# RWKV-7 state scan and hash-routed experts on one core: identity taken out of u, own and ends moved to GpSimd, routing moved to the last ticks

## The chip, the core and the metric

The kernel runs on one NeuronCore of a Trainium2 chip. A core has five engines with queues of their own: TensorE (PE in the profile, with its weight loads as PEld), VectorE (DVE), ScalarE (ACT), GpSimd (POOL) and SyncE (SP, which here only issues DMA transfers). Each works through its instructions in order; an instruction that waits holds everything behind it on the same engine. The metric is device time in microseconds; smaller is better.

## What is computed

An RWKV-7 recurrence over 768 steps for 4 x 8 heads of size 40, then an expert layer in which each token goes to one of eight experts by a hash of its id.

```python
for t in range(S):
    y[:, :, t] = np.einsum('bhd,bhde->bhe', rt, state)
    Sa = np.einsum('bhde,bhe->bhd', state, at)
    state = state * wt[:, :, None, :] - np.einsum('bhd,bhe->bhde', Sa, bt)
    state = state + np.einsum('bhd,bhe->bhde', vt, kt)
...
expert_idx = token_ids * 2654435761 % E
for e in range(E):
    mask = expert_idx == e
    out[mask] = np.maximum(x[mask] @ w1[e], 0.0) @ w2[e]
```

The state starts at zero. x is y with the heads of a token side by side: 3072 tokens of 320 values. Everything is float32.

## The kernel before

**Tiles.** The sequence is cut into 12 chunks of 64 steps. A tile is one chunk of two of the four batches: 24 tiles, numbered u, alternating between two states (g = u mod 2). Partitions 0-63 hold one batch's 64 steps, 64-127 the other's. Inside a chunk the recurrence is solved by matrix products. Products of w (the decays) scale a, b, k and r; a_ps holds the products of a with b and k; a unit triangular 64 x 64 system per head is inverted. It is split in two blocks of 32 (BLK): the diagonal blocks of four tiles (a group) are inverted together on DVE, column by column (31 steps of two instructions, outer and ub), and the off-diagonal block comes from two small matmuls, x (from ut, a transposed copy of the inverse) and u (from ug, another one).

**The order.** Each piece of work is a function with a tick, a number. The plan is sorted by tick and emitted in that order; an order written by hand decides each engine's queue. Tile u is prepared at ticks up to u+1 (tile_a: loads, multiplication by decays, transposes z_ps and t_ps, a_ps) and finished at tick u + LAG, LAG being 8 (tile_m, tile_s, tile_b). Within a tick the steps are c, u, rcc, nc, rcv, z, s, a, sd, x, r0, at_t, r1, y, rv. So one tick finishes tile k and prepares tile k+8; from tile 16 on only finishing is left.

**The steps that matter here.**
- x_ps (tile_m) goes to xi by ACT. xi also holds a 32 x 32 identity, written once at the start (L212), so that the u matmul, with 64 stationary columns, gives both the off-diagonal block and a copy of ug. ACT copies u_ps to um (L647) and writes the first half of um as ug times the mask first (L651).
- c_ps = r1 times um; cv is its copy (ACT, L721); rc needs cv; ACT's copy rv (L687) stands ahead of cv. nc transposes cv and gives x_all (L749).
- r0 (tile_b) adds the old state sc to r1; s adds it to the new state through an identity matmul, y adds it through sd. DVE makes sc from s_ps (L765), mr from rc_ps (L738), xs from y_ps (L782). For the first tile of each state sc and sd are zero, set on POOL (L166).
- Matmul results lie in PSUM: two buffers in turn (psa) for c, rc, z, a, sd and the transposes, two others (psb) for u, nc, s, x, r1, y, ex, en. A step waits until the reader of the step two before it in its pair is done.
- The decays are made in rounds (ri) of two chunks by decays(): clamp (L302, DVE), prefix and suffix products (on POOL from round 1), own (L312, L314: the product of a half chunk, DVE), ex_ps (PE: exchange of halves), ends (L334, DVE), recip (L341), spread (L345, POOL), and the transposes qt and pt (L349, DVE).
- routing() is a generator called in steps from tick 11.5 on, 0.42 apart: load of the token ids (tok, L828), counts by two matmuls (sums_ps), ranks and slots on DVE, 24 indirect scatters into slot_dram (POOL, L910), the read back to idx_all, and src_all on DVE. The first gather of the expert stage needs src_all and all x_rows.
- py (the decay product per row) is loaded and x_rows stored on POOL's queue, except the stores of the last two tiles, which are on SP.

Of the kernel before, what the change touches and what calls it, by code (L numbers as in the profile page):

```python
# [18 lines left out]
def kernel(  # L19
# [13 lines left out]
    nc = tc.nc  # L33
# [141 lines left out]
    for lo, hi, when in ((0, 4, -9.0), (4, NZ, -3.0)):  # L175
        @at_tick(when)
        def _(lo=lo, hi=hi):
            nc.gpsimd.memset(z_all[:, lo:hi].rearrange("p i b hp (two x) -> p (i b hp two) x", two=2)[:, :, D:C], 0.0)
# [8 lines left out]
    r_r = ring("r", 2, [P, HP, P], gaps)  # L187
    x_all = hold.tile([P, 3, 2, HP, P], F32, name="x_all")
    @at_tick(-3.0)
    def _():  # L190
        nc.gpsimd.memset(x_all[:].rearrange("p i b hp (two x) -> p (i b hp two) x", two=2)[:, :, D:C], 0.0)
    e2_r = ring("e2", 2, [P, R], lambda t: t.rearrange("p (two x) -> p two x", two=2)[:, :, D:C], 1)
    sd_r = ring("sd", NG, [R, 2, HP, 2, D], all_of)
    sc_r = ring("sc", NG, [R, 2, HP, 2, C], all_of)
    pend_r = ring("pend", NR, [P, RN, NG, 2, HP, 2], all_of, NR)
    nk = hold.tile([P, LAG, 2, 2, HP, C], F32, name="nk")
    xi_r = ring("xi", 1, [P, H, C])
# [9 lines left out]

    @at_tick(-8.95)
    def _():
        for be in range(2):  # L210
            rows = slice(be * C + BLK, (be + 1) * C)
            nc.scalar.copy(xi_r(0)[rows, :, BLK:C], ident[rows, rows].unsqueeze(1).to_broadcast([BLK, H, BLK]))  # L212
# [67 lines left out]
    def decays(ri, t_load, t_clamp, t_chain, t_own, t_ex, t_ends, t_pair, t_recip, t_en, t_spread, t_turn):  # L280
# [3 lines left out]
        chain = nc.vector if fast else nc.gpsimd  # L284

        for i in range(4 * RN):
            @at_tick(t_load + (0.06 * i if ri > 2 else 0))
            def _(i=i):
# [6 lines left out]
                eng = nc.scalar if fast and n % 2 else nc.sync  # L295
                r0 = (y * RN + n) * NG * H
                dma = eng.dma_start(x["pb"][r0:r0 + NG * H], src)
# [11 lines left out]
        def own():  # L309
            p, q = segs(x["pb"]), segs(x["qb"])  # L310
            x["own"] = own = work.tile([P, SEG, D], F32, tag="own", name="own", bufs=2)
            nc.vector.tensor_tensor(own[:], p[:, :, SL - 1], q[:, :, SL - 1], op=OP.mult)  # L312
            for s in range(SEG - 2, -1, -1):
                nc.vector.tensor_tensor(own[:, s], own[:, s], own[:, s + 1], op=OP.mult)  # L314
# [17 lines left out]
        def ends():  # L332
            ends = x["ends"]
            nc.vector.tensor_tensor(ends[:, 0:SEG], x["own"][:], ends[:, SEG].unsqueeze(1).to_broadcast([P, SEG, D]), op=OP.mult)  # L334
# [113 lines left out]
    def tile_a(u):  # L448
# [8 lines left out]
        if early:  # L457
            t_in, t_inz = -8.9 + 0.01 * u, -8.9 + 0.01 * u if u < 3 else -8.45
            t_mul = -6.0 + 0.01 * u
            t_mulz = -6.1 + 0.01 * u if u < 2 else t_mul - 0.005  # L460
            t_z, t_at, t_a = u - 0.3, (-0.15, 0.5, 0.95, 1.0)[u], u + 0.9 if u < 3 else u + 0.4
# [70 lines left out]
        def _():  # L532
# [9 lines left out]
            if u > GRP - 2:  # L542
                nc.scalar.copy(both, p[:])  # L543
                for be in range(2):
                    low = slice(be * C + BLK, (be + 1) * C)
                    nc.scalar.copy(nk[low, u % LAG, :, 0, :, 0:BLK], p[low, :, 0:HP * C].rearrange("p two (hp t) -> p two hp t", hp=HP)[..., BLK:])
# [24 lines left out]
    def group_i(gi, t0, t1, t2, t3):  # L571
# [38 lines left out]
        @at_tick(t3, order=9)  # L610
        def _():
            ub = x["u"]
            x["ug"] = ug = work.tile([P, BLK, BLK], F32, tag="ug", name="ug", bufs=1)
            nc.vector.transpose(ug[:].rearrange("p g t -> p t g"), ub[:].rearrange("p s t -> p t s"))
# [5 lines left out]
    def tile_m(u, t0):  # L620
# [5 lines left out]
        def _():  # L626
# [7 lines left out]
            for be in range(2):  # L634
                low = slice(be * C + BLK, (be + 1) * C)
                nc.scalar.copy(xi[low, :, 0:BLK], p[low])

        @at_tick(t0 - 1, "u")
        def _():
            ug, xi = groups[gi]["ug"], x["xi"]  # L640
            p = bank([P, H, BLK], "u_ps")
            for hp, par, be in quarters():
                h = hx(par, hp)
                low = slice(be * C + BLK, (be + 1) * C)
                mm(p[half(be), h, :], xi[low, h, :], ug[low, ti * H + h, :])
            x["um"] = um = work.tile([P, H, C], F32, tag="um", name="um", bufs=1)
            nc.scalar.copy(um[:, :, BLK:C], p[:])  # L647

        @at_tick(t0 - 0.7 if u else t0 - 0.93)
        def _():  # L650
            nc.scalar.mul(x["um"][:, :, 0:BLK], groups[gi]["ug"][:, ti * H:(ti + 1) * H, :], first[:, 0:1])  # L651

    def tile_s(u, t0):
# [20 lines left out]
        def _():  # L674
            x["py"] = py = work.tile([P, DM], F32, tag="py", name="py", bufs=1)
            cols = slice((rn * NG + g) * H, (rn * NG + g + 1) * H)
            nc.gpsimd.dma_start(py[:], p_dram[ri][:, cols].rearrange("t c e -> t (c e)"))
# [11 lines left out]
    def tile_b(u, t0):  # L689
# [5 lines left out]
        @at_tick(*((t0 - 1, "r0") if u else (6.56,)))  # L695
        def _():
            x["r1_ps"] = p = bank([P, DM], "r1_ps")
            for hp in range(HP):
                for be in range(2):
                    c0 = hp * 2 * D  # L700
                    mm(p[half(be), c0:c0 + 2 * D], x["at_t"][0:R, be, hp, :], st[:, be, hp, :, 0:D],
                       start=hp == 0, stop=False)

        @at_tick(*((t0 - 1, "r1") if u else (6.57,)))
        def _():
            p = x.pop("r1_ps")
            for hp, par, be in quarters():
# [3 lines left out]
                   start=False)  # L711
# [39 lines left out]
        if not last:  # L751
            @at_tick(t0, "s")
            def _():
# [3 lines left out]
                for par in range(2):  # L757
                    mm(p[half(par)], ident[half(par), half(par)], sc[half(par), :, :, par, 0:D], stop=False)
                for hp, par, be in quarters():
                    mm(p[half(par), be, hp * D:(hp + 1) * D], x["z"][:, be, hp, half(par)], x["x"][:, be, hp, half40(par)],  # L760
                       start=False)
# [8 lines left out]
        def _():  # L770
            p = bank([P, DM], "y_ps")
            for hp in range(HP):
# [4 lines left out]
            for hp, par, be in quarters():  # L777
                c0 = (2 * hp + par) * D
                mm(p[half(be), c0:c0 + D], x["mr"][:, par, hp * 2 + be, :],
                   x["z"][:, be, hp, par * C:par * C + D], start=False)  # L780
            xs = work.tile([P, DM], F32, tag="xs", name="xs", bufs=1)
            nc.vector.tensor_tensor(xs[:], p[:, 0:DM], x["py"][:], op=OP.mult)  # L782
            for be in range(2):
                r0 = batch(g, be) * S + n * C
                (nc.sync if last else nc.gpsimd).dma_start(x_rows[r0:r0 + C, :], xs[half(be)])  # L785
# [14 lines left out]
    decays(1, -8.5, -7.09, (-7.08, -7.0), 0.85, 0.91, 0.92, 1.2, 0.93, 3.6, 0.95, (3.445, 2.0))  # L800
    decays(2, -5.5, 3.45, (5.61, 5.9), 6.2, 6.555, 6.56, 6.57, 6.561, 8.2, 6.58, (7.62, 7.55))
    for ri in range(3, NR):
        t = ri * RN * NG
        decays(ri, t - 5.8, *((7.75, (8.3, 8.9), 8.95) if ri == 3 else (t - 5.2, (t - 5.1, t - 3.9), t - 3.55)), t - 2.9, t - 2.89, t - 2.6, t - 2.45, t - 1.88, t - 2.4, (t - 0.9, t - 1.48))
# [5 lines left out]
    for gi in range(NU // GRP):  # L810
# [3 lines left out]
        else:  # L814
            group_i(gi, t0 + 0.03, t0 + 0.06, t0 + 2.68, t0 + 2.97)
# [126 lines left out]
    for i in range(14 + TPP):  # L942
        at_tick(11.5 + 0.42 * i, order=7)(lambda: next(steps, None))
# [287 lines left out]
```

## Time and profile before

| | us |
|---|---|
| runs | 716.06, 719.69, 712.3 (median 716.06) |
| the profiled execution | 702.85 |
| its span, first to last instruction | 701.1 |
| granted TensorE clock, mean | 0.932 |

| engine | busy us | share of the span |
|---|---|---|
| PE | 606.5 | 87% |
| DVE | 357.3 | 51% |
| ACT | 262.8 | 37% |
| POOL | 269.2 | 38% |

The first c_ps matmul starts at 85.7 us and the last tile's at 425.6. The first matmul of the expert stage proper (up_ps) is at 445.2; from there to the end PE is busy 243 of 256 us. Busy shares are averages over a head in which the first inverse has to be finished, the ticks, and the expert stage, so they are to be read stretch by stretch. The clock column is the granted TensorE clock in that stretch, 1.00 being full speed: at 0.5 a matmul takes up to twice as long.

### The profile page before, as it was taken

To read this page: it belongs to the slowest core of one execution; us is meant where nothing else is said; L and a number is where in the kernel's file an instruction comes from. 1 tells how busy PE (TensorE), PEld (TensorE's weight loads), DVE (VectorE), ACT (ScalarE), POOL (GpSimd) and SP (SyncE) were. 2 spreads that over 40 slices of the span, in tenths; PEclk is the share of its full clock that TensorE was granted. 3 is DMA by queue.
4 is the path that set the end of the run, shared out by engine and by line. 5 is a ranking of instruction groups with operands and counts; after the bars stand their busy time and mean duration, and the time that the engine had idled before them with its cause. 6 is when DMAs were issued, how large, how long until landed. Compare 5 with 4: busy or idle time off the path is not lost.

```text
span 701.1 us, 23965 instructions
## 1 busy us (share of the span) xinstructions
PE 606.5 (87%) x10442; PEld 455.0 (65%) x10442; DVE 357.3 (51%) x759; ACT 262.8 (37%) x520; POOL 269.2 (38%) x343
## 2 busy tenths in 40 slices
PE   0446678989999999989989994899999999999995
PEld 0335657877878888878878884364656556565653
DVE  6969797858988966873676313328111111111110
ACT  2576434754566657555534541111111111111110
POOL 2569367574637785454331111312213030210101
PEclk9988568997999999998989998699999999999999
DMA  9874053554555756774434522896322442120000
GB/s 136 157 114 113 2 105 78 116 123 91 110 110 114 133 101 102 131 136 66 80 55 82 117 55 73 297 339 217 102 73 87 145 149 85 46 93 20 28 5 29
DMA packets 163517, 73.86 MB, mean 105 GB/s; under 512 B 136078, under 2 KB 157135, under 8 KB 163408
## 3 DMA queue, kind: packets, MB, share of 16 engines
q1 hardware_dynamic: 153232, 55.55, 36.6%
q0 software_dynamic: 5824, 15.75, 8.4%
q10 hardware_dynamic: 4352, 0.98, 1.2%
q8 instruction: 83, 1.36, 0.9%
q14 instruction: 26, 0.21, 0.1%
HBM read 56.73 MB, written 12.16 MB: 98 GB/s over the span
## 4 chain that ended last, share of the span: by engine, by line
PE 39%; issue 33%; DVE 12%; POOL 6%; DMA 5%; SPq 2%; ACT 1%; POOLq 0%; DVEq 0%; ACTq 0%
PE r_ps L242 5%; PE y_ps L242 5%; PE s_ps L242 5%; PE rc_ps L242 4%; PE u_ps L242 4%; DVE ub L603 3%; DVE outer L600 3%; POOL out_dram L1030 3%; PE sd_ps L562 3%; PE a_ps L242 2%; PE z_ps L562 2%; POOL xg L1000 2%; PE t_ps L567 2%; PE nc_ps L747 2%; PE x_ps L242 2%
## 5 line engine op out<-in xcount | busy, mean ns | idle before, releaser
L1040 PE MATMUL dn_ps<-w,ht 128*128 128x320 f32 x384 | 104.9, 433 | 0.0
L1030 POOL DMA_INDIRECT out_dram<-o,idx_all x26 | 25.7, 990 | 185.4 <-ACT o L1029 178.6
L1020 PE MATMUL up_ps<-xt,w 128*128 128x416 f32 x256 | 94.0, 520 | 0.0
L1040 PEld LDWEIGHTS dn_ps<-w,ht 128*128 128x128 f32 x384 | 72.8, 190 | 32.1 <-issue 2.4
L1020 PEld LDWEIGHTS up_ps<-xt,w 128*128 128x128 f32 x256 | 47.5, 191 | 46.0 <-issue 46.0
L785 POOL DMA_DIRECT2D x_rows<-xs x44 | 24.5, 561 | 115.6 <-DVE xs L782 77.1
L603 DVE TENSOR_TENSOR ub<-ub,outer 128x31 f32<-128x31 f32 (+15 forms) x186 | 65.0, 349 | 6.3
L600 DVE TENSOR_TENSOR outer<-ub,nb 128x31 f32<-128x31 f32 (+15 forms) x186 | 62.7, 337 | 7.4 <-ACT ub L583 2.8
L1023 DVE TENSOR_SCALAR ht<-up_ps 128x416 f32<-128x416 f32 x32 | 18.9, 591 | 92.4 <-PE up_ps L1020 92.4
L1006 DVE COPY xt<-xg_ps 128x384 f32<-128x384 f32 x24 | 12.1, 551 | 83.4 <-PE xg_ps L1005 83.4
L562 PE MATMUL z_ps<-ident,z_all 128*128 128x128 f32 x192 | 32.0, 318 | 24.0 <-POOL z_all L499 10.7
L1029 ACT COPY o<-dn_ps 128x320 f32<-128x320 f32 x24 | 10.2, 426 | 101.6 <-PE dn_ps L1040 101.6
L738 DVE TENSOR_TENSOR mr<-rc_ps,after 128x1024 f32<-128x1024 f32 x24 | 29.2, 1218 | 29.3 <-PE rc_ps L242 29.3
L562 PEld LDWEIGHTS z_ps<-ident,z_all 128*128 128x128 f32 x192 | 24.9, 162 | 27.8 <-POOL z_all L499 11.9
L499 POOL TENSOR_TENSOR z_all<-z_all,qt 128x320 f32<-128x320 f32 x40 | 34.4, 872 | 13.0 <-DMA z_all<-in_k_dram 9.1
L687 ACT COPY rv<-t_ps 128x1024 f32<-128x1024 f32 x24 | 24.3, 1012 | 39.6 <-PE t_ps L567 39.6
L1025 ACT ACTIVATE ht<-up_ps 128x416 f32<-128x416 f32 x32 | 15.9, 514 | 60.8 <-PE up_ps L1020 60.8
L1000 POOL DMA_INDIRECT xg<-x_rows,src_all x26 | 25.5, 982 | 32.3 <-PE xg_ps L1005 17.5
L242 PE MATMUL u_ps<-ug,xi 32*64 32x32 f32 x768 | 30.6, 228 | 5.5 <-issue 2.7
L749 ACT COPY x_all<-nc_ps 64x512 f32<-64x512 f32 x44 | 25.6, 581 | 25.0 <-PE nc_ps L747 24.5
L543 ACT COPY nk<-a_ps 128x1024 f32<-128x1024 f32 x21 | 21.3, 1013 | 33.8 <-PE a_ps L242 33.4
L1016 PE MATMUL up_ps<-xt,w 64*128 64x416 f32 x128 | 28.4, 562 | 6.3 <-DVE xt L1006 3.9
(186 smaller groups left out, 1192.2 us busy)
## 6 DMA issues: line engine op xcount, KB each, us to landing
w<-in_moe_w_dram SPq DMA_DIRECT2D x7, 1280.0 KB, 7.1
w<-in_moe_w_dram SPq DMA_DIRECT2D x7, 1024.0 KB, 5.4
r<-in_r_dram SPq DMA_DIRECT2D x48, 80.0 KB, 3.9
x_all<-in_v_dram SPq DMA_DIRECT2D x48, 80.0 KB, 2.9
py<-p_rows POOLq DMA_DIRECT2D x24, 160.0 KB, 3.3
wt<-in_w_dram SPq DMA_DIRECT2D x24, 160.0 KB, 7.3
z_all<-in_b_dram SPq DMA_DIRECT2D x46, 80.0 KB, 2.9
z_all<-in_k_dram SPq DMA_DIRECT2D x46, 80.0 KB, 3.3
```

What stands on the lines that cost most here:

```text
L242: pe_last[0] = nc.tensor.matmul(out_, lhsT=lhsT, rhs=rhs, start=start, stop=stop, skip_group_check=True).ins
L499: eng.tensor_tensor(t, t, by.rearrange("p (h e) -> p h e", e=D), op=OP.mult)
L562: pe_last[0] = nc.tensor.transpose(dst, src, ident[:]).ins
L600: nc.vector.tensor_tensor(tv, ub[:, 0:j + 1, j:j + 1].to_broadcast([P, j + 1, m]), nb[:, j, j + 1:].unsqueeze(1).to_broadcast([P, j + 1, m ...
L603: nc.vector.tensor_tensor(o, o, tv, op=OP.add)
L738: nc.vector.tensor_tensor(t[:].rearrange("p two h t -> p (two h) t"), p[:].rearrange("p two (h t) -> p (two h) t", t=C), after[:].unsqueez ...
L749: nc.scalar.copy(x["x"][half(be), be], p[half(be)])
L1000: g = nc.gpsimd.indirect_dma_start(out=xg[:, 0:DM], out_offset=None, in_=x_rows[:], in_offset=bass.IndirectOffsetOnAxis(ap=idx, axis=0))
L1016: nc.tensor.matmul(banks[-1][:], lhsT=w1(f, 2), rhs=xt[part(f), 2, 0:n], start=True, stop=False)
L1020: nc.tensor.matmul(p[:], lhsT=w1(f, c), rhs=xt[:, c, 0:n], start=False, stop=(c == 1))
L1030: st = nc.gpsimd.indirect_dma_start(out=out[:], out_offset=bass.IndirectOffsetOnAxis(ap=idx, axis=0), in_=o[:], in_offset=None, bounds_che ...
L1040: nc.tensor.matmul(p[:], lhsT=ht[:, f, j * P:(j + 1) * P], rhs=w2(f), start=(f == 0), stop=(f == FP - 1))
```

## The change

It has six parts.
- u loses its identity: xi holds only the off-diagonal part (32 columns). ug is gone; DVE transposes the inverse straight into um, a tile of a whole group with one buffer, and ACT fills the masked half by one multiplication for four tiles. The u matmul writes 32 partitions per batch, and two ACT copies put the result over the upper half of um's second part. The transpose into um is at the tick in which the last tile of the group before has been used (group 0: at once). For the first tile of a group after the first, u moves from just behind c to behind z.
- own and ends of rounds 2 to 5 run on GpSimd. In rounds 3 to 5 they and the exchange are 0.1 to 0.3 of a tick later, and PE meets ex_ps after s.
- routing runs from tick 25.0, 0.1 apart, its scatters from 26.4, 0.14 apart. py and x_rows of tiles 16 to 23 go on SP's queue.
- The first tile of each state skips r0, the identity part of s, and the sd part of y.
- Zero sets on GpSimd are earlier; sd has none, sc only its gaps.
- Smaller: the low block of nk is copied from nk in SBUF instead of from PSUM; z of tile 1 is transposed earlier in the plan; the transposes of round 1's pt are at another tick.

```diff
-    sd_r = ring("sd", NG, [R, 2, HP, 2, D], all_of)
-    sc_r = ring("sc", NG, [R, 2, HP, 2, C], all_of)
+    sd_r = ring("sd", NG, [R, 2, HP, 2, D])
+    sc_r = ring("sc", NG, [R, 2, HP, 2, C], lambda t: t.rearrange("p b h two x -> p (b h two) x")[:, :, D:C], NG)
...
-    xi_r = ring("xi", 1, [P, H, C])
+    xi_r = ring("xi", 1, [P, H, BLK])
...
-    @at_tick(-8.95)
-    def _():
-        for be in range(2):
-            rows = slice(be * C + BLK, (be + 1) * C)
-            nc.scalar.copy(xi_r(0)[rows, :, BLK:C], ident[rows, rows].unsqueeze(1).to_broadcast([BLK, H, BLK]))
...
+        eng = nc.vector if ri < 2 else nc.gpsimd
...
-            nc.vector.tensor_tensor(own[:], p[:, :, SL - 1], q[:, :, SL - 1], op=OP.mult)
+            eng.tensor_tensor(own[:], p[:, :, SL - 1], q[:, :, SL - 1], op=OP.mult)
             for s in range(SEG - 2, -1, -1):
-                nc.vector.tensor_tensor(own[:, s], own[:, s], own[:, s + 1], op=OP.mult)
+                eng.tensor_tensor(own[:, s], own[:, s], own[:, s + 1], op=OP.mult)
...
-            nc.vector.tensor_tensor(ends[:, 0:SEG], x["own"][:], ends[:, SEG].unsqueeze(1).to_broadcast([P, SEG, D]), op=OP.mult)
+            eng.tensor_tensor(ends[:, 0:SEG], x["own"][:], ends[:, SEG].unsqueeze(1).to_broadcast([P, SEG, D]), op=OP.mult)
...
-                    nc.scalar.copy(nk[low, u % LAG, :, 0, :, 0:BLK], p[low, :, 0:HP * C].rearrange("p two (hp t) -> p two hp t", hp=HP)[..., BLK:])
+                    nc.scalar.copy(nk[low, u % LAG, :, 0, :, 0:BLK], nk[low, u % LAG, :, 0, :, BLK:])
...
-            x["ug"] = ug = work.tile([P, BLK, BLK], F32, tag="ug", name="ug", bufs=1)
-            nc.vector.transpose(ug[:].rearrange("p g t -> p t g"), ub[:].rearrange("p s t -> p t s"))
+            x["um"] = um = work.tile([P, BLK, C], F32, tag="um", name="um", bufs=1)
+            nc.vector.transpose(um[:, :, BLK:].rearrange("p g t -> p t g"), ub[:].rearrange("p s t -> p t s"))
+
+        @at_tick(6.97 if gi == 0 else t3 + 0.005, order=9)
+        def _():
+            um = x["um"]
+            nc.scalar.mul(um[:, :, 0:BLK], um[:, :, BLK:], first[:, 0:1])
...
-        @at_tick(t0 - 1, "u")
+        @at_tick(*((t0 - 0.62,) if u and ti == 0 else (t0 - 1, "u")))
...
-                mm(p[half(be), h, :], xi[low, h, :], ug[low, ti * H + h, :])
-            x["um"] = um = work.tile([P, H, C], F32, tag="um", name="um", bufs=1)
-            nc.scalar.copy(um[:, :, BLK:C], p[:])
+                top, low = slice(be * C, be * C + BLK), slice(be * C + BLK, (be + 1) * C)
+                mm(p[top, h, :], xi[low, h, :], um[low, ti * H + h, BLK:])
+            for be in range(2):
+                top = slice(be * C, be * C + BLK)
+                nc.scalar.copy(um[top, ti * H:(ti + 1) * H, BLK:], p[top])
...
-            nc.gpsimd.dma_start(py[:], p_dram[ri][:, cols].rearrange("t c e -> t (c e)"))
+            (nc.sync if u >= NU - LAG else nc.gpsimd).dma_start(py[:], p_dram[ri][:, cols].rearrange("t c e -> t (c e)"))
...
-                for par in range(2):
+                for par in range(2 if n else 0):
                     mm(p[half(par)], ident[half(par), half(par)], sc[half(par), :, :, par, 0:D], stop=False)
...
-            for hp in range(HP):
+            for hp in range(HP if n else 0):
...
-                (nc.sync if last else nc.gpsimd).dma_start(x_rows[r0:r0 + C, :], xs[half(be)])
+                (nc.sync if u >= NU - LAG else nc.gpsimd).dma_start(x_rows[r0:r0 + C, :], xs[half(be)])
...
-        decays(ri, t - 5.8, *((7.75, (8.3, 8.9), 8.95) if ri == 3 else (t - 5.2, (t - 5.1, t - 3.9), t - 3.55)), t - 2.9, t - 2.89, t - 2.6, t - 2.45, t - 1.88, t - 2.4, (t - 0.9, t - 1.48))
+        decays(ri, t - 5.8, *((7.75, (8.3, 8.9), 8.95) if ri == 3 else (t - 5.2, (t - 5.1, t - 3.9), t - 3.55)), t - 2.6, t - 2.59, t - 2.5, t - 2.45, t - 1.88, t - 2.4, (t - 0.9, t - 1.48))
...
-            group_i(gi, t0 + 0.03, t0 + 0.06, t0 + 2.68, t0 + 2.97)
+            group_i(gi, t0 + 0.03, t0 + 0.06, t0 + 2.68, gi * GRP + LAG - 0.99)
...
-        at_tick(11.5 + 0.42 * i, order=7)(lambda: next(steps, None))
+        at_tick(25.0 + 0.1 * i if i < 14 else 26.4 + 0.14 * (i - 14), order=7)(lambda: next(steps, None))
```

## The prediction

> **What bounds the kernel now.** I read the busy time of each engine in stretches cut at the first matmul of c_ps of each tile (stretch k, or tick k below, runs from tile k to tile k+1), then the chain of waits inside the long stretches, then the timeline around one tick, then groups by tile.
>
> ```profile
> 85.66:110.50 24.84, 19.68 (x398) 16.19 (x394) 19.08 (x39) 11.31 (x25) 15.27 (x24) 0.69 0.40 82
> 110.50:128.31 17.81, 15.31 (x407) 13.15 (x405) 14.79 (x32) 9.28 (x19) 12.53 (x10) 0.90 0.47 99
> 142.28:158.77 16.49, 14.61 (x403) 12.53 (x401) 10.53 (x18) 9.22 (x16) 13.19 (x23) 1.00 0.60 124
> 158.77:177.65 18.88, 17.73 (x399) 14.87 (x396) 14.80 (x41) 8.84 (x15) 7.67 (x10) 0.73 0.42 86
> 255.58:269.55 13.97, 13.97 (x400) 12.03 (x398) 10.80 (x18) 10.12 (x21) 7.57 (x9) 1.00 0.61 92
> 360.51:372.07 11.56, 11.14 (x324) 9.69 (x321) 10.21 (x25) 5.39 (x10) 4.66 (x6) 1.00 0.61 88
> 395.53:406.60 11.07, 11.07 (x323) 9.69 (x321) 2.54 (x3) 5.39 (x10) 1.62 (x3) 1.00 0.32 64
> ```
>
> Columns: stretch, length, busy PE, PEld, DVE, ACT, POOL, clock, DMA share, GB/s. A clean tick is PE from end to end (13.97 of 13.97; 11.07 of 11.07 once no new tiles are prepared). Ticks 0, 1, 3 and 4 are 24.84, 17.81, 16.49 and 18.88 long: something else holds PE, and the clock falls to 0.69-0.73. After 445 us the expert stage takes 256 us; the change does not touch it. So all is decided before 445 us: in the head up to tile 6, where other engines lead, and in stretches 16-18, where DVE is nearly as full as PE.
>
> ```profile
> 39.47 1.79 POOL sc L166 x2
> 80.55 0.16 DVE ends L334
> 80.74 0.35 ACT e L338 x2
> 82.44 2.31 PE u_ps L242 x32
> 153.85 2.25 DMA tok<-in_moe_token_ids_dram
> 180.20 2.47 DVE ends L334
> 190.16 2.41 DVE ovt L872
> ```
>
> The chain (start, us, what) names the holders: zero sets on POOL at 39, an end product at 80 with the first u behind it, the token load at 153, long DVE instructions at 180-192.
>
> ```profile
> L314 DVE TENSOR_TENSOR own<-own x18: 199/200/2653, 12.1 to 233.3; 128x40 f32<-128x40 f32 x18
> L334 DVE TENSOR_TENSOR ends<-own,ends x6: 289/322/2560, 14.0 to 240.1; 128x160 f32<-128x160 f32 x6
> ```
>
> Minimum, median, maximum in ns: own and ends are short alone and 2.5 us when POOL is in its 2.9 us multiply (L345).
>
> ```profile
> 344.78 0.69 PE L242 MATMUL c_ps<-um,r 64*64 64x64 f32 x32
> 344.89 1.01 ACT L687 COPY rv<-t_ps 128x1024 f32<-128x1024 f32 x1 [1.90 <-PE t_ps L567]
> 345.41 1.12 PE L242 MATMUL u_ps<-ug,xi 32*64 32x32 f32 x32
> 345.80 0.59 ACT L721 COPY cv<-c_ps 128x512 f32<-128x512 f32 x1
> 346.46 0.69 PE L242 MATMUL rc_ps<-rv,cv 64*64 64x64 f32 x32
> 427.30 0.69 PE L242 MATMUL rc_ps<-rv,cv 64*64 64x64 f32 x32 [1.02 <-ACT cv L721]
> ```
>
> This decides what a shorter u is worth. rc needs cv; ACT makes cv only after rv, at 346.39; rc starts at 346.46, when u has just ended. u is a cover over the copy. Tile 23 has no u behind its c, and PE sits 1.02 us.
>
> **Part 1, u.** The 16 matmuls (32 records) lose the identity half: 64 stationary columns become 32, as in x_ps, whose 32 records take 0.63 us at full clock where u takes 1.05. The rule that speaks here is the Trainium skill's "TensorEngine Tiling (Array Packing)", Instruction Overhead: each matmul has a fixed cost of about 60 cycles, and a factor isn't to be taken from a dimension already small; with moving size 32 as before, u would not shrink at all. I take the row (0.63). With the row, an ordinary tick gains only rc's slack over cv: 0.05-0.07 us in most, 0.3 in ticks 2, 5, 9, 10: about 1 us in all (by the rule 0). In the five ticks in which a group starts (3, 7, 11, 15, 19) u is moved behind z: PE now waits the bare 1.02 us for cv and pays u later, so 1.02 - 0.42 = 0.6 lost each, 3 us (by the rule 5). In 3, 7 and 11 DVE also has the 1.95 us transpose into um (it must wait for c of the previous group's last tile, um having one buffer) and three quarter transposes (1.18 each) ahead of mr: 0.7 + 1.95 + 3.5 + 1.2 = 7.4 after c, and a_ps, due at 7.0 in the slot that mr frees, waits about 0.5: 1.5 us. On ACT the eight 0.51 multiplies of two groups become two of 1.01, and one 0.37 copy becomes two of 0.36: hidden, ACT is 9 of 14 busy; without that cover 0.1 us a tick. Reading nk from SBUF instead of PSUM: 0.36 to 0.40 (the xi row of SBUF source), hidden alike. Net of part 1: -1 + 3 + 1.5 = +3.5.
>
> **Part 2, the head.** sd's sets (1.2) are gone, sc's shrink, all sit before 10 us where POOL idles until 24.7. The identity copies into xi (2 x 0.40) leave ACT ahead of its first loads; DVE's first clamp (7.14) waits for w, so 0; the table load moves to about 12, ahead of the copies at 13.3 that need it, and tile 1's z ahead of its at trades one in-order wait for another: 0 each. Then POOL's qb multiply starts with ends and recip, about 37.6 instead of 41.22; DVE's qt and pt, now ahead of the third nk, need not be interleaved with it: after nk (42.2) come 2.7 + 2.7 + 0.7 + 2.1 + 0.7, so the inverse starts near 51.1 instead of 52.6: 1.5. Round 2's own (0.9, in the middle of the inverse) leaves DVE: ut ends at 76.3 instead of 78.8; um's transpose at 78.3. ACT is no longer held at e and rv. u runs 78.4-79.4 (half clock), its copies to 80.2, c of tile 0 near 80.5 instead of 85.66: 5.1 us. ACT's ub set, which holds the next inverse, moves from 85.5 to 80.2. In stretch 0 DVE stays the bound up to mr (99.0 before, 94.2 after); past it tile 1 has no old state, so r0 no longer waits for sc (1.71) nor runs (1.33), and y loses 0.8: another 2.6. In stretch 1 own (0.32 + 3.12) leaves DVE, and with it PE's 2.47 us gap before ex_ps, half-clock window included; s and y shorten by 1.0: 17.8 to about 12.4, 5.4. On POOL the added work is 4 x (0.56 + 3 x 0.25 + 0.56), estimated from L307's 0.556 for 160 elements; it fills gaps before x_rows; ex_ps needs own only after s. Bounds: 0 to 1 us a round; I take 0. Sum of part 2: 13.
>
> **Part 3, routing moved.** Removed from ticks 3-6: the stop for tok, the 2.41 us ovt, ends at 2.47. Against a 14.0 tick: 16.49, 18.88, 15.39 and 16.77 give back 2.5 + 4.9 + 1.4 + 2.8 = 11.6. The 4.9 is half clock: after gaps of 1.85 and 1.15 us the clock was half for 10.2 us. "TensorE: Matmul & The Clock Gate" (what's actually happening) has PE throttled after an idle window of 3.4 us, which no gap here fills; I follow the trace.
>
> Added in stretch 17, with DVE already 10.2 of 11.56: from xs of tile 16 (359.65 = 0), two x_rows issues now on SP, then tok, which lands at 4.0; eid and mine to 5.0; PE, with sums queued before rc, waits 2.8. DVE then has two inverse steps, scan (1.3), mr, two sums (0.7), two steps, so sc ends near 12.5-13.9 where it was 8.3; eight more routing bunches with five steps (8.5) put xs of tile 17 at 21-22 instead of 11.5, and nc waits for its bank; key_i, the last steps, ut, mr, sc follow, and r0 of tile 20 comes at 29-30 instead of 20.6: 9 lost, 10 with one half-clock window that DVE's lead does not cover. By the page's rule it is 9.
> On SP, the py and x_rows issues of the last eight tiles stand ahead of r and v loads with two ticks of reserve: 0 (the last v load stands behind idx_all, with about 12 us of reserve). The 24 scatters run alone on POOL:
>
> ```profile
> 436.90 0.97 POOL L1000 DMA_INDIRECT xg<-x_rows,src_all  x1 [0.31 <-issue]
> 438.18 0.94 POOL L1000 DMA_INDIRECT xg<-x_rows,src_all  x1 [0.30 <-issue]
> ```
>
> Such issues repeat every 1.27 us. The fill lands at 26.5, scatters end at 57, land by 60; idx_all takes 6.5 from issue to src_all (376.57 to 383.08): 66.5. On DVE xs of tile 21 is queued behind src_all, due at 67: 0, with 3 us to spare.
>
> **Sum.** +3.5 - 13 - 11.6 + 10 = -11. The profiled execution took 702.85 (span 701.1): 692. The median shown is 716.06, 13 above it; the same step gives **705**.
>
> **Rivals.**
> *No change.* The head is in-order on four engines; half of the 13 goes where nothing shows it now (POOL holding ex_ps, recip waiting for POOL's ends, a load landing late), or the half clock in stretches 17-18 lasts as long as after tok, 10 us: about 712. For it: each repair above opens a new last wait within 1-2 us. Against: the 11.6 of ticks 3-6 leaves with its instructions.
> *Slower.* The chain tok, mine, key, scatters, idx_all, src_all ends last, and xs, nc and the gathers hang on it. Its end is 36.5 + 24 x T after xs of tile 16; above T = 1.38 us every microsecond costs one. At T = 2.1 it costs 18, the total becomes +7: 723. For: scatters landed 2.3-5.8 us after issue. Against: with POOL otherwise idle T was 1.27.
> *Not what it says:* u really is halved and the orders really move in the built program; but "u without identity" bringing PE time is refuted above, and without the rest the kernel would stand at 719.
>
> **Numbers.** Forecast 0.58 (697 to 709), no change 0.27 (709 to 723), slower 0.15 (723 up; about 1% is what a measurement can tell here). Range 696 to 718: one in ten beyond each end.
>
> **What would show it.** Right: c_ps of tile 0 near 80.5, of tile 2 near 115-117, of tile 7 near 186 (209.8 before); no DVE own over 1 us after 40 us; rc waiting for cv about 0.4 us in every tick, 1.0 in five; then eid waiting for tok near 4 us after xs of tile 16 and stretches 17-18 together about 10 longer. Wrong: ex_ps or recip waiting for POOL in ticks 1, 5, 9; u still at 1.05; c_ps of tile 7 later than 200; src_all later than xs of tile 21 could start.

## The result, and the profile after

The changed kernel takes 746.06 us (median of 4 runs, 743.97 to 746.65), the kernel before 714.18 beside it (4 runs, 707.79 to 719.69): a ratio of 1.047 (95% interval 1.039 to 1.055), slower. The forecast was 705. The profiled execution after spans 744.8 us, the one before 701.1, which was one of the fastest of its kernel: of the 43.7 between the two profiles some 11 is that luck (702.85 against a median of 714.18).

Where it went, in the prediction's stretches (stretch k from the first c matmul of tile k to that of tile k+1; 23 to the first up_ps):

| Part of the span | Before | Forecast of the change | After | Change |
|---|---|---|---|---|
| start of c of tile 0 | 85.7 | -5.1 | 81.5 | -4.2 |
| stretches 0 and 1 | 42.6 | -8.0 | 34.4 | -8.2 |
| 3, 7, 11, 15 (a group starts) | 57.8 | +1.4 | 81.2 | **+23.5** |
| 4, 5, 6 | 51.0 | -9.1 | 41.6 | -9.4 |
| 2, 8-10, 12-14, 16 | 123.4 | -1 | 109.7 | **-13.6** |
| 17 and 18 | 23.8 | +10 | 62.0 | **+38.2** |
| 19 to 23 | 60.9 | +0.6 | 66.1 | +5.2 |
| expert stage | 255.9 | 0 | 268.3 | **+12.4** |

The same view as before, busy time by stretch (stretch, length, busy PE, PEld, DVE, ACT, POOL with instruction counts, clock, DMA share, GB/s), of the changed kernel, for stretches 0, 1, 4, 7, 18 and 20:

```profile
81.47:103.19 21.72, 17.84 (x362) 15.63 (x357) 19.99 (x40) 11.59 (x26) 14.65 (x21) 0.55 0.47 93
103.19:115.86 12.67, 12.33 (x387) 10.88 (x384) 11.45 (x27) 8.97 (x19) 12.16 (x18) 1.00 0.64 130
149.26:163.09 13.83, 13.50 (x399) 11.60 (x396) 11.85 (x30) 8.64 (x15) 8.99 (x14) 1.00 0.59 122
190.90:212.36 21.46, 15.92 (x399) 13.59 (x396) 11.77 (x18) 10.84 (x18) 11.82 (x20) 0.84 0.44 93
365.99:410.37 44.38, 18.16 (x325) 13.77 (x320) 9.69 (x32) 5.11 (x10) 23.98 (x27) 0.63 0.15 31
426.23:437.24 11.01, 10.67 (x325) 9.25 (x320) 2.54 (x3) 5.11 (x10) 0.00 (x0) 1.00 0.32 63
```

The head (first two lines) and the ticks that lost the routing (third) are as short as forecast. In stretch 7 PE is busy 15.92 of 21.46. In stretch 18 it is busy 18.16 of 44.38, and POOL 23.98: that is 24 scatters, and hardly anything else moves (31 GB/s).

**The group starts.** PE, ACT and DVE around the start of stretch 3 of the changed kernel, from the timeline (start, us, engine, line, what; in brackets the idle time before it and what ended it):

```profile
129.83 0.69 PE L236 MATMUL c_ps<-um,r 64*64 64x64 f32 x32
130.68 1.90 DVE L609 STREAM_TRANSPOSE um<-ub 128x1024 f32<-128x1024 f32 x1 [0.32 <-PE c_ps L236]
132.61 1.01 ACT L577 COPY ub<-upper 128x1024 f32<-128x1024 f32 x1 [4.56 <-DVE um L609]
133.66 0.19 ACT L578 COPY ub<-ones 128x32 f32<-128x32 f32 x1
133.78 1.01 ACT L685 COPY rv<-t_ps 128x1024 f32<-128x1024 f32 x1
134.68 0.59 ACT L720 COPY cv<-c_ps 128x512 f32<-128x512 f32 x1
135.32 1.13 PE L236 MATMUL rc_ps<-rv,cv 64*64 64x64 f32 x32 [4.80 <-ACT cv L720]
```

It is one chain. The transpose into um waits for c of the previous group's last tile, which still reads the one um buffer; ACT's fill of ub, for the next inverse, waits for that transpose; and the copies of rv and cv stand behind the fill on ACT's in-order queue. So PE waits 4.80 us for cv, and its next matmuls take 1.1 instead of 0.7: half clock (0.5 granted from 135.0 on, for 3.4 us).

**The scatters.** PE and POOL in the middle of stretch 18, timeline of the changed kernel:

```profile
388.84 0.35 PE L236 MATMUL y_ps<-z_all,mr 128*64 128x40 f32 x2 [1.76 <-issue]
389.56 0.22 PE L236 MATMUL y_ps<-z_all,mr 128*64 128x40 f32 x1 [0.37 <-issue]
390.96 0.23 PE L236 MATMUL y_ps<-z_all,mr 128*64 128x40 f32 x1 [1.18 <-issue]
391.69 0.23 PE L236 MATMUL y_ps<-z_all,mr 128*64 128x40 f32 x1 [0.50 <-issue]
...
389.41 0.98 POOL L909 DMA_INDIRECT slot_tokens<-token,key_i  x1 [0.30 <-issue]
390.70 0.98 POOL L909 DMA_INDIRECT slot_tokens<-token,key_i  x1 [0.30 <-issue]
391.98 0.98 POOL L909 DMA_INDIRECT slot_tokens<-token,key_i  x1 [0.30 <-issue]
```

PE waits for no engine ("issue" is time for which the profile shows no cause). In these lines one or two matmuls start every 0.7 or 1.4 us (elsewhere in the stop up to 2.8 us pass), where 32 of them take 1.08 undisturbed. It begins at 377.7, 2.5 us after the first scatter, and ends at 409.3, 4.5 after the last began. PE's waits from 376 to 412 (in all, times, longest):

```profile
PE y_ps L236 <- issue: 19.9, 23, 2.5
PE t_ps L562 <- issue: 3.5, 3, 1.9
```

**The end.** The drains at the end of the program, view by source line, before (first line) and after:

```profile
L1226 POOLq DRAIN  x3: 40/109/1954, 698.3 to 700.8; - x3
```
```profile
L1225 POOLq DRAIN  x3: 40/109/10202, 733.8 to 744.5; - x3
```

Minimum, median and maximum in ns: POOL's last long drain takes 10.2 us instead of 1.95. From the last scatter of output rows to the end it was 6.8 us (694.3 to 701.1) and is 16.1 (728.7 to 744.8). The other 3.1 of the expert stage lies in its first two experts.

### The profile page after: what moved, and what is told of

Read it like the earlier page. It is cut to its first block, busy times and chain, and to the rows that moved or that the text cites. A ratio compares the mean times of both kernels' runs of the same rounds, so it can differ in the third digit from the quotient of the medians.

```text
span 744.8 us, 23843 instructions
## 1 busy us (share of the span) xinstructions
PE 599.0 (80%) x10370; PEld 445.4 (60%) x10370; DVE 345.0 (46%) x739; ACT 264.3 (35%) x524; POOL 261.7 (35%) x341
## 4 chain that ended last, share of the span: by engine, by line
PE 35%; issue 34%; DVE 10%; ACT 5%; POOL 5%; DMA 5%; SPq 3%; POOLq 0%; DVEq 0%; ACTq 0%
PE y_ps L236 5%; PE r_ps L236 5%; PE s_ps L236 4%; PE rc_ps L236 4%; POOL out_dram L1029 3%; PE z_ps L557 3%; DVE ub L598 3%; DVE outer L595 3%; PE sd_ps L557 3%; PE a_ps L236 2%; ACT rv L685 2%; POOL xg L999 2%; PE t_ps L562 2%; PE nc_ps L746 2%; PE x_ps L236 2%
## 5 line engine op out<-in xcount | busy, mean ns | idle before, releaser
L1028 ACT COPY o<-dn_ps 128x320 f32<-128x320 f32 x24 | 10.2, 425 | 101.6 <-PE dn_ps L1039 101.6
L236 PE MATMUL y_ps<-z_all,mr 128*64 128x40 f32 x768 | 30.7, 229 | 19.2 <-issue 18.6
L781 DVE TENSOR_TENSOR xs<-y_ps,py 128x320 f32<-128x320 f32 x24 | 11.7, 488 | 66.3 <-remote 33.9
L784 POOL DMA_DIRECT2D x_rows<-xs x32 | 17.9, 562 | 69.7 <-DVE outer L595 42.8
L236 PE MATMUL rc_ps<-rv,cv 64*64 64x64 f32 x768 | 20.0, 252 | 26.2 <-ACT cv L720 26.0
L557 PEld LDWEIGHTS z_ps<-ident,z_all 128*128 128x128 f32 x192 | 25.8, 166 | 24.6 <-POOL z_all L494 11.5
L236 PEld LDWEIGHTS y_ps<-z_all,mr 128*64 128x64 f32 x768 | 27.6, 140 | 20.5 <-issue 19.6
L909 POOL DMA_INDIRECT slot_tokens<-token,key_i x24 | 23.6, 982 | 41.5 <-DVE mr L737 34.5
```

The source lines that it names most:

```text
L236: pe_last[0] = nc.tensor.matmul(out_, lhsT=lhsT, rhs=rhs, start=start, stop=stop, skip_group_check=True).ins
L557: pe_last[0] = nc.tensor.transpose(dst, src, ident[:]).ins
L909: st = nc.gpsimd.indirect_dma_start(out=slot_dram[:, None], out_offset=bass.IndirectOffsetOnAxis(ap=key_i[:, c:c + 1], axis=0), in_=token[ ...
```

## The experiments

Three losses are to be explained: the group starts, stretch 18, the end. "The changed kernel" is the start of each edit unless another is named. Times are medians where there were several runs; ratios are to the kernel before on the same chip (709.5 to 712.9).

**The group starts**

```diff
-        @at_tick((-7.45, 7.3)[gi] if gi < 2 else t0 - 0.62, order=9)
+        @at_tick((-7.45, 7.3)[gi] if gi < 2 else t0 - 0.2, order=9)
```

> One number of the changed kernel is moved: ScalarE's fill of ub is put behind the copies of rv and cv (0.2 of a tick ahead of its group's start instead of 0.62). Theory: in the ticks that start a group (stretches 3, 7, 11 and 15) the fill waits for the transpose of ub into um, and the copies of rv and cv are queued behind it, so that PE waits 4.8 to 5.5 us at rc and cools. Then the waits at rc fall to about 1 us, the four stretches from 19.5, 21.5, 20.4 and 19.9 to about 14.2 each, and the kernel takes about 722 instead of 746. Rival: the one um tile, which must be read out by the c of the last tile before it can be written, sets the wait by itself; then the four stretches keep at least 17.5 and the kernel takes 738 or more.

721.76, ratio 1.016 (1.005 to 1.026). The timeline at the same place:

```profile
129.64 0.70 PE L236 MATMUL c_ps<-um,r 64*64 64x64 f32 x32
131.30 0.69 PE L236 MATMUL rc_ps<-rv,cv 64*64 64x64 f32 x32 [0.96 <-ACT cv L720]
```

The four stretches take 14.88, 14.68, 14.69 and 14.25. The order of one fill on ACT was worth 24 us. With it right, the wait for cv is the bare one of the prediction (0.96; 1.02 was forecast), and the four stretches stand 0.7 above those before, where 1.4 was forecast.

**The routing back**

```diff
-        at_tick(25.0 + 0.1 * i if i < 14 else 26.4 + 0.14 * (i - 14), order=7)(lambda: next(steps, None))
+        at_tick(11.5 + 0.42 * i, order=7)(lambda: next(steps, None))
```

> The changed kernel with the routing's steps back at ticks 11.5 to 27 (0.42 of a tick apart) as before the change; all else as changed. Theory: the 24 scatters stall PE while they follow one another, about 1.3 us for each, and less where they lie apart: stretches 16 to 19, together 90.9 now, come to 50 to 54; the earlier stretches take back about 20 in all (the routing's own steps 11 and scatters that lie apart 0.3 to 0.5 each); the kernel takes about 728. Rival: the loss in stretch 18 comes from the late x_rows and p loads that now stand on SP's queue, and not from the scatters: stretches 16 to 19 stay over 80, and the kernel takes 755 or more.

727.57, ratio 1.019 (1.009 to 1.029). Stretches 16 to 19 take 52.6 (90.9 as changed), though x_rows and p are still on SP.

**The scatters left out**

```diff
-            st = nc.gpsimd.indirect_dma_start(
-                out=slot_dram[:, None],
...
-            tc.add_to_no_dep_group("slots", st.ins)
```

> The changed kernel with the 24 scatters into slot_tokens left out (every slot then keeps the fill value, so that each gather reads the last row and no result row is written; the expert stage is not compared, only what lies ahead of it). Theory: the scatters stall PE: stretch 18 falls from 44.4 to 12 to 14 and stretch 19 from 15.9 to 11 to 12; the start of the expert stage comes some 35 to 38 us sooner. Rival: PE lacks something else there (the loads of r, v and the first weights that SP issues in the same microseconds): stretch 18 stays over 35.

Stretches 17 to 19 take 17.83, 16.62 and 12.58. Stretch 18 has lost 28 of its 44, and the expert stage starts 28 us sooner (35 to 38 were expected: a half-clock window stays in stretch 18). What is left in 17 and 18, 34.5 against 23.8 before the change, is the price of the rest of the routing: +10.7 (+8.1 in the run with reads, next). That it is its DVE work is argued from the waits, of which the longest, 3.3 us, is for DVE's mine; it was not taken out by itself.

**Reads in place of the writes**

```diff
-                out=slot_dram[:, None],
-                out_offset=bass.IndirectOffsetOnAxis(ap=key_i[:, c:c + 1], axis=0),
-                in_=token[:, c:c + 1], in_offset=None, bounds_check=NT * P - 1, oob_is_err=False)
+                out=got[:, c:c + 1], out_offset=None, in_=slot_dram[:, None],
+                in_offset=bass.IndirectOffsetOnAxis(ap=key_i[:, c:c + 1], axis=0))
```

> The changed kernel with each of the 24 scatters put as an indirect read of the same 128 words of 4 bytes from slot_tokens into SBUF (the slots keep their fill value, so the expert stage is not compared). Theory one: what stalls PE is GpSimd's indirect form, reads as well as writes: stretch 18 stays over 35. Theory two: it is the small writes to DRAM: stretch 18 takes 12 to 18, as without the scatters (16.6).

One run, 718.56. Stretch 18 and the issues in it:

```profile
367.56:381.29 13.73, 10.79 (x310) 9.09 (x302) 8.68 (x28) 5.11 (x11) 4.64 (x5) 1.00 0.43 100
```
```profile
376.78 0.97 POOL L910 DMA_INDIRECT got<-slot_tokens,key_i  x1 [0.30 <-issue]
378.06 0.94 POOL L910 DMA_INDIRECT got<-slot_tokens,key_i  x1 [0.30 <-issue]
```

The same row of issues at nearly the same pace (1.25 us), and the clock stays at 1.00: neither POOL's making of indirect descriptors nor its being busy stalls PE. The writes to DRAM do. Over stretches 17 to 22 PE's waits with the cause "issue" come to 23.3 us in the changed kernel, and there is none without scatters or with reads.

**Plain writes, from POOL and from SP**

```diff
+            st = nc.gpsimd.dma_start(slot_dram[c * P:(c + 1) * P].unsqueeze(1), token[:, c:c + 1])
```
(`nc.sync` in the second)

> The changed kernel with each of the 24 scatters put as a plain transfer from GpSimd's queue: the same 128 words of 4 bytes, to 128 places in a row of slot_tokens instead of places read from key_i (the order of the tokens is then not the reference's). Theory one: what stalls PE is the transfer of 128 words of 4 bytes issued by GpSimd, whatever its addresses: stretch 18 stays over 35. Theory two: it is the indirect form (addresses worked out from an index tile): stretch 18 falls to 12 to 16.

> The changed kernel with the 24 scatters put as plain transfers of the same 128 words of 4 bytes on SP's queue, none on GpSimd's (the order of the tokens is then not the reference's). Theory one: it is GpSimd's making of descriptors that stalls PE: stretches 18 to 20 take together 40 to 44, as without the scatters (40.2). Theory two: it is the small writes themselves, whoever issues them, since with plain transfers from GpSimd a fetch of instructions took 5.7 us instead of 1 and PE stood for 7.9: stretches 18 to 20 take 52 or more.

From POOL (one run, 732.81) stretches 18 to 20 take 13.8, 29.5 and 15.6, together 58.8; from SP (one run, 747.6) 57.7, where 40.2 is left without writes. SP's writes go on until 433.8, and stretches 21 and 22 take 37.5 there instead of 19.0, so the whole loss is 36 us (in part waits for DVE, 4.5 us, and half clock). The first expectation looked at the wrong stretch: stretch 18 is clean, and 19 holds the loss. PE in it, with plain writes from POOL:

```profile
379.37 0.68 PE L236 MATMUL c_ps<-um,r 64*64 64x64 f32 x29
387.95 0.48 PE L236 MATMUL c_ps<-um,r 64*64 64x64 f32 x3 [7.89 <-issue]
```

c stops after 29 matmuls for 7.89 us. The packet records show that a fetch of 16,384 bytes of instructions (there is one for some 250 instructions of PE), which takes about 1 us elsewhere, began at 377.9 here and took 5.7; with the writes on SP those at two stops of PE took 3.4 and 4.1. So small writes stall PE whoever issues them, and here some of its fetches are slow. That the slow fetch is the cause of the stop is not shown: here it had ended 4.3 us before c went on, with the writes on SP PE went on at 382.7 while the fetch of 3.4 us still ran, and in two runs below (the routing late on the kernel before, and with all queues on POOL) fetches of 2.9 to 3.9 us have no stop over 1.7 us near them. The Trainium skill ("Runtime: NRT & Kernel Launch", Instruction fetch mechanics) has instructions streamed in blocks of this size while the block before is worked off, mostly hidden; the block size is this trace's, and whether the hiding fails here stays open. A slow fetch doesn't explain stretch 18 of the changed kernel, where the one fetch inside the stall (at 378.9) took 0.96.

**Both edits, and the queues of the last eight tiles**

```diff
-            (nc.sync if u >= NU - LAG else nc.gpsimd).dma_start(py[:], p_dram[ri][:, cols].rearrange("t c e -> t (c e)"))
+            nc.gpsimd.dma_start(py[:], p_dram[ri][:, cols].rearrange("t c e -> t (c e)"))
...
-                (nc.sync if u >= NU - LAG else nc.gpsimd).dma_start(x_rows[r0:r0 + C, :], xs[half(be)])
+                (nc.sync if last else nc.gpsimd).dma_start(x_rows[r0:r0 + C, :], xs[half(be)])
```
The first run has neither line, the second the first, the third both.

> The changed kernel with both edits: ScalarE's fill of ub behind rv and cv, and the routing back at ticks 11.5 to 27. Theory: the two losses lie in different stretches and add up: stretches 3, 7, 11 and 15 (22.0, 20.5, 19.9 and 21.9 with the routing back alone) come to 15 to 17, and the kernel takes about 706. GpSimd's drain at the very end still takes 10.2. Rival: with the routing's DVE work in these ticks the transpose into um is late anyway, and the four stretches stay over 18.5: 718 or more.

> As the run before it, and the eight last p loads back on GpSimd's queue: 132 transfers on that queue instead of 124. In the profiled runs GpSimd's drain after its last transfer took 10.2 us at 124 transfers, 8.24 at 100 and 1.95 at 144: 0.082 for each transfer, counted anew after some 121. Theory: the drain follows that count, so it takes about 1 us here, and the kernel about 9 less than the run before it. Rival: the drain grows with what SP's queue carries or with what else was moved: it takes 6 to 10 us here.

> As the run before it, and the x_rows writes of the last eight tiles back on GpSimd's queue as before the change (144 transfers). Theory: the drain takes 1.95 as before the change, the rest is as in the run before it: about 697, which would be 2 per cent under the kernel before. Rival: without the routing moved late, nothing is left of the gain at the head once the group starts are paid: 708 or more.

705.29, ratio 0.994 (0.989 to 0.999); 694.82, ratio 0.985 (0.975 to 0.994); 696.39, ratio 0.982 (0.973 to 0.992). The drains (by source line; POOL's lines of the second of these and of the run without scatters):

```profile
L1225 POOLq DRAIN  x3: 40/109/1056, 693.6 to 695.2; - x3
```
```profile
L1219 POOLq DRAIN  x3: 40/109/8242, 709.0 to 717.8; - x3
```

POOL's transfers and its long drain, over the profiled runs: 100, 8.24; 124, 10.20; 132, 1.06; 144, 1.95. The 1 us for 132 was forecast before its run. All 17 profiled runs show one of these four pairs. The run with plain writes on SP has 24 transfers more on SP's queue than the run without scatters and the same 100 on POOL's, and the drain is 8.24 in both: it follows POOL's count, not SP's. Between 100 and 124 it grows by 0.08 us for each transfer, somewhere between 124 and 132 it drops, and up to 144 it grows again, like a sawtooth; where it drops, and whether it does so again, was not measured. Moving 20 transfers to SP put the kernel at the highest of the four counts; with eight transfers back, the last expert's stretch is 10.6 us shorter (38.6 instead of 49.2).

**The queues alone, with the routing late**

> The changed kernel with the p loads and x_rows writes of the last eight tiles back on GpSimd's queue, nothing else. The scatters stay in the last ticks, but the queue holds them in groups of seven or fewer with a wait for a tile's xs between them, as in the kernel before with the routing late, where stretches 18 to 22 took 72. Theory one: PE is starved only while scatters follow one another without a break; on SP's queue the other transfers no longer break the row. Then stretches 18 to 22, 90.2 as changed, come to 68 to 75, the drain takes 1.95 instead of 10.2, and the kernel takes about 719. Theory two: each of the 24 scatters costs its 1.3 us wherever it is: stretches 18 to 22 stay over 84, and only the drain's 8 are won: about 737.

> As the run before it, with ScalarE's fill of ub late as well; the routing stays in the last ticks. Theory one: the two add up: about 695 to 699, no slower than the kernel with the routing spread over ticks 11.5 to 27 (695 and 696). Theory two: about 713.

732.65, ratio 1.036 (1.025 to 1.047), and 709.40, ratio 1.007 (1.004 to 1.010). The drain is 1.95 in both. But stretches 18 to 22 take 95.1 and 87.1, not 68 to 75: POOL's own x_rows and p now break the scatters into groups of seven and fewer, and each group stalls PE again (16.1 us of "issue" waits in 25 over stretches 17 to 22). What is left of the gain is the end of the program. With the fill late, late routing is 13 us slower (709.4) than routing spread over the middle ticks (696.4).

**The same row on the kernel before** (the routing line above put into the kernel before)

> The kernel before with the routing's steps alone moved to the last ticks, as in the change; all transfers on their old queues. Theory: the 24 scatters in a row stall PE here too, about 1.3 us each, and the x_rows and p transfers of the last tiles queue behind them on GpSimd; some 20 come back in the earlier ticks and at the single gaps: net 15 to 35 slower than before (725 to 747). Rival: without the changed kernel's other edits the late ticks hold the routing for nothing: within 5 of before.

711.03, ratio 1.003 (0.999 to 1.007). The rival's number came, but not for its reason: stretches 3 to 16 give back 19.7 and 17 to 22 lose 20.1. The same groups of seven cost less here than in the run before (3.9 us of "issue" waits against 16.1). Why was not found out.

**Scatters with pauses**

```diff
             tc.add_to_no_dep_group("slots", st.ins)
+            for _ in range(14):
+                nc.gpsimd.memset(pause[:], 0.0)
```

> The changed kernel with fourteen small fills by GpSimd (some 1.3 us of its time) after each scatter: a scatter every 2.6 us instead of every 1.28, other transfers as changed, on SP's queue. The scatters then end about 31 us later, so the total is not compared. Theory one: the unbroken row starves PE: with gaps between them the stretches they touch (18 to 22) lose less than 12 in all against those without scatters (59.2 in the run that left them out), so under 71. Theory two: each scatter costs 1.3 us: those stretches together stay over 84.

The fills took 2.9 us, so a scatter went every 4.4. Stretches 18 to 21:

```profile
365.05:378.82 13.77, 10.88 (x324) 9.28 (x321) 9.63 (x32) 5.11 (x10) 3.39 (x16) 1.00 0.42 100
378.82:392.71 13.89, 11.29 (x324) 9.56 (x321) 4.51 (x4) 6.36 (x11) 9.86 (x46) 1.00 0.45 76
392.71:404.37 11.66, 11.03 (x324) 9.49 (x321) 2.45 (x3) 5.11 (x10) 8.34 (x43) 1.00 0.46 59
404.37:416.27 11.90, 11.40 (x322) 9.72 (x321) 2.05 (x2) 5.23 (x10) 8.25 (x38) 1.00 0.28 52
```

Together 51.2; without scatters it was 51.3 (some of that at half clock), with reads 48.8. Some ten scatters with pauses cost 2.5 us at most, at full clock; "issue" waits are 1.4 us in all. (Stretch 22, 77 us, then waits for the fill of the slots to end, which comes later here; so 18 to 22 can't be compared as a whole, and the total, 780.5 in one run, not at all.) In these stretches it is the row that stalls PE, not the single scatter.

**Two other places for the routing**, both on the version of 694.82

```diff
-    for i in range(14 + TPP):
-        at_tick(11.5 + 0.42 * i, order=7)(lambda: next(steps, None))
+    for t in ([-9.01] + [-8.4 + 0.03 * i for i in range(11)] + [-7.5 + 0.001 * i for i in range(15)]
+              + [3.40 + 0.001 * i for i in range(5)] + [6.9 + 0.001 * i for i in range(4)] + [9.1, 9.6, 9.9]):
+        at_tick(t, order=7)(lambda: next(steps, None))
```
(in the first, the load of the token ids is also a step of its own and DVE copies the counts; the second has `[11.5 + 0.42 * i for i in range(11)] + [21.0 + 0.34 * i for i in range(TPP)] + [29.4, 30.6, 30.8]`, and eight fills after each of the last sixteen scatters)

> As the run with the fill late, the routing at ticks 11.5 to 27 and the p loads on GpSimd's queue (695), but with the whole routing at the head: the token ids loaded first, its DVE steps while DVE waits for the first loads, and the 24 scatters in GpSimd's idle stretches (15 ahead of the second round's decays, 5 ahead of the products of the second four tiles, 4 at the end of the head), where PE mostly waits for others; the counts come out of PSUM by DVE instead of ScalarE. Theory: scatters cost PE time wherever PE is the bound, even when they lie apart. Then stretches 3 to 19, together 260 in that run, come to about 230, c of tile 0 comes 4 to 7 later than its 80.8, and the kernel takes about 671. Rival: scatters that lie apart cost next to nothing, and the surplus in those stretches is DVE's and the transposes': they stay over 250, and with the head's loss the kernel takes 690 or more.

> As the run with the fill late, the routing from tick 11.5 and the p loads on GpSimd's queue (694.8; its stretches 3 to 19 took 260 where about 230 is left without routing), but the scatters from tick 21 on, 0.34 of a tick apart, and eight small fills by GpSimd (about 1.8 us) after each of the last sixteen, so that no two follow each other at once. Theory one: only rows of scatters, and single ones beside heavy loads in the middle ticks, starve PE; apart, in the late ticks, they cost next to nothing, as where they were 4.4 us apart. Then the routing's DVE steps are left, about 10: stretches 3 to 19 come to 238 to 246, and the kernel takes 674 to 683. Theory two: the surplus of 30 in the middle ticks is DVE's: stretches 3 to 19 stay over 252, the kernel over 690.

At the head: 706.64, ratio 0.998 (0.994 to 1.002). Stretches 3 to 19 did fall to 233, so routing in the middle ticks costs about 27. But c of tile 0 comes at 99.3, 18.6 later, and stretch 2 grew to 26.4. DVE's first routing step ran into POOL's zero sets:

```profile
3.82 4.76 DVE L835 TENSOR_SCALAR eid<-tok 128x24 int32<-128x24 int32 x1 [2.59 <-DMA tok<-in_moe_token_ids_dram]
```

It took 0.18 us in the changed kernel and 4.76 here. Two DVE steps behind it, 0.29 each there, took 4.7 and 4.5; all three ended at 8.58, and the last of POOL's sets at 8.55. The 15 early scatters then held POOL's second-round decays until 47. Apart in the late ticks: 696.27, ratio 0.977 (0.961 to 0.992), within the noise of 694.82. Stretches 3 to 19 take 258.8, as theory two said, but not for its reason: stretches 9, 11 and 14 became 7.1 shorter, and 13, 16 and 19 7.4 longer, so the loss went along with the scatters. Near those from tick 21 on, among loads, PE has stops of 2.9, 2.3 and 2.4 us, with half clock after the first and the last. The first began 4 us after one scatter and 2.3 before the next, so that the single scatter is its cause is not shown. Pauses made scatters free in one place and not in another; what else must hold is open.

## Why the prediction was wrong

**Part 2, the head, held**: c of tile 0 at 81.5 (80.5 forecast), of tile 2 at 115.9 (115 to 117), no own or ends on DVE after 39 us, and PE between 95 and 340 us waits for cv and hardly anything else (next fence): 12.4 won, 13 forecast. Inside the sum two terms differ: the first inverse starts at 52.3 here, 0.2 sooner where 1.5 was forecast (at 50.2 to 52.3 over the profiles with this head), and from the end of ut to c 3.1 was won, where 2.6 was forecast. One reading of the prediction was off: no slow own or ends of DVE ran beside POOL's multiply L345; those of 2.65 and 2.56 us (111.9 and 180.1) ran beside its multiplies L499 and L558. The repair does not depend on which.

The waits of PE over that window of the changed kernel (in all, times, longest):

```profile
PE rc_ps L236 <- ACT cv L720: 22.7, 12, 5.5
PE t_ps L557 <- DVE mr L737: 0.8, 1, 0.8
PE u_ps L236 <- issue: 0.3, 1, 0.3
```

**Part 1 held for u, failed at the group starts.** u's 32 records take 0.69, near the row of x_ps (0.63) and not the unchanged 1.05 that the prediction drew from the Trainium skill's fixed cost of a matmul ("TensorEngine Tiling (Array Packing)", Instruction Overhead), and in ordinary ticks rc waits 0.34 for cv, so a shorter u buys next to nothing there. The step that failed is "PE now waits the bare 1.02 us for cv and pays u later, so 1.02 - 0.42 = 0.6 lost each". It followed the late transpose into um to DVE's next work (mr) and not to the other engine that waits for it: ACT's fill of ub, with rv and cv behind it. The waits were 4.8 to 5.5, and the four stretches lost 23.5 where 1.4 was forecast. The run with the fill late shows that this was the whole of it.

**Part 3 held for DVE, failed for the scatters.** With the fill late, ticks 3 to 6 give back 11.0 (11.6 forecast). Stretches 17 and 18 lose 10.7 without scatters (10 forecast). The step that failed is "scatters end at 57, land by 60 ... 0, with 3 us to spare". The pace was right (1.28 us), and the rival "slower" had put its price on that pace; it was never the pace. That the measured time lies where this rival put it is luck: the chain that it named held nothing (stretch 22 takes 7.92, as before). The row itself keeps PE from issuing: 28 us in stretch 18, 3 in 19. The profile before had a mark of it, gaps of PE with the cause "issue", and the sum took no account of them:

```profile
249.00 0.43 PE L242 MATMUL x_ps<-ut,nk 32*32 32x32 f32 x14 [1.38 <-issue]
316.14 0.42 PE L242 MATMUL u_ps<-ug,xi 32*64 32x32 f32 x3 [1.70 <-issue]
```

Stretches 3 to 16 have five over 0.4 us. Three stand at scatters (242.3, 300.1, 314.4); the first one shown has none within 4 us. But they go with the routing's place: the six profiled runs whose scatters lie in these stretches have two to nine such gaps each, and the eleven others have one between them. Read as a price of the routing there, they would also have pointed at the second gain that the forecast lacks, 13.6 in the ordinary ticks, all of it in 9, 12 to 14 and 16. The after profile has none of them there; that they make up all of the 13.6 is not shown.

**The transfers moved to SP: "0" was right for SP, and missed POOL.** The price, 9.3 us, lies at the end of the program.

**The clock.** In the version of 694.82 a gap of 1.79 us at 287.1 is followed by 6.8 us at half clock, and one of 1.06 at 257.8 by 3.4; with the routing apart, a gap of 2.25 at 323.0 is followed by none. The rule of the Trainium skill ("TensorE: Matmul & The Clock Gate", What's actually happening: throttled after an idle window of about 3.4 us) fits the waits of 4.8 and more and not these. The measured rows decide; no threshold comes out of them.

## What to carry to other kernels

When an instruction gets a new wait, list every engine that waits for its result, and on each of them what stands behind that waiter: here a fill that nobody needed for 14 us held two copies that PE needed at once. A row of small writes to DRAM is not free because its queue is idle: look in the profile at hand for "issue" gaps beside such writes, and don't let them follow one another; what distance is enough was not settled. Of several edits the good ones can be kept: the head won 12 us here, and with the fill late and the routing and the queues put back the kernel runs at 0.98 of the one before.

## What the hardware showed

- With indirect writes of 128 words of 4 bytes to DRAM from POOL, one transfer every 1.28 us, PE issued mostly one or two matmuls every 0.7 to 2.8 us; with reads of the same words every 1.25 us it lost nothing, and with such writes every 4.4 us 2.5 us at most in four stretches.
- Under plain writes of that size some of PE's instruction fetches took 3 to 5.7 us instead of about 1, and PE stood for up to 7.9; that the one makes the other is not shown.
- POOL's drain at the end of the program follows the number of transfers on its queue: 8.24 us at 100, 10.20 at 124, 1.06 at 132, 1.95 at 144.
- Beside POOL's zero sets of SBUF a DVE step took 4.76 us instead of 0.18 and ended with the last set (one run).
- Not settled: by what path the row holds PE in the changed kernel, where its fetch took 0.96 us, and why groups of seven (with the routing's DVE work) lengthen stretches 17 to 22 by 43 us in the changed kernel with all transfers on POOL, and by 20 in the kernel before.
